# Attention in blocks of 64 tokens from the second batch on, another way out for the last outputs, and other priorities in the planner

## The chip, the cores and the metric

The kernel runs on one core of a Trainium2 chip. The core has a matrix engine (TensorE, PE in the rows; its weight loads are PEld), VectorE (DVE), ScalarE (ACT), GpSimd (POOL) and SyncE (SP), which issues transfers. Matrix products go to banks of PSUM, everything else is in SBUF. The metric is the device time of one launch in microseconds, on random inputs of the fixed shapes below. Lower is better.

## What is computed

Four batches of 768 tokens. A linear attention with decay over 8 heads of 48 gives x (384 columns), which goes through two small networks in a row. Cut to its core:

```python
# attention, per token t, state [B, H, 48, 48]
cur = einsum('bhd,bhe->bhde', u * k_t, v_t)
y_t = einsum('bhd,bhde->bhe', r_t, state + cur)
state = w[..., None] * state + einsum('bhd,bhe->bhde', k_t, v_t)
# first network
h = gelu(x @ w_in)                       # [B, 768, 1024]
u, v = h[..., :512], h[..., 512:]
v_n = layernorm(v) * g_ln
v_s = einsum('ts,bsd->btd', w_sg, v_n) + b_sg[None, :, None]
x2 = x + (u * v_s) @ w_out
# second network, conv over 5 tokens back
gate = sigmoid(sum(conv_w[k] * x2_padded[:, k:k+768] for k in range(5)))
out = (gate * (x2 @ w_val)) @ w_out2
```

## The kernel before

**Attention** goes through 24 chunks of 128 tokens (i = 0 to 23, six to a batch, NCH = 6). r is multiplied by the decay up to its token, k by its inverse, both are transposed (att_T, tiles rT and kT), then scores kT x rT are made and masked so that only earlier tokens count, and scores x v plus state x r give y. The term of the token itself, with u, is dv, a multiple of v. There are two forms of a chunk.

- *Plain* (i < QUAD = 12): scores for 128 tokens (L680) into two PSUM banks, masked by DVE (L690, two instructions) into two buffers "sc"; in att_Y the transpose of dv (L858), state x r (L864) and v x scores (L877) into one bank, copied out by ScalarE (L902); KV for the next state (L707), added by DVE (L716, L718).
- *In blocks of 64 tokens* (i >= QUAD): att_Yq makes state x r and v x scores (L842) for two half chunks in two banks, and at once the scores (S_blocks, L751) and KV (KV_blocks, L785) of the next chunk in two more. The diagonal with u is put into the score tile beforehand, and DVE copies the scores over it under a mask (L759, two instructions); y is copied out of two banks (L936) and two additions by DVE bring the parts together (L942). The states are then three tiles T2, which `states` lays into the two "sc" buffers once chunk QUAD - 1 is done, with memsets on GpSimd.

For chunks up to RAW - 1 = 12 r and k are transposed by TensorE (L654) into one bank each, and emptied by DVE (rT, L662) and ScalarE (kT, L660). From chunk 13 on DVE transposes them (L622).

**The networks** are lists of tasks per batch (V, U: the two halves of w_in with gelu; S: gate product with w_sg; O: w_out; A: w_val; P: w_out2). Every product is done three times with parts of high and low order (L1093, L1094, L1095). The weights come as double words and are made into such parts by `prepare`: a load by SP (L391), ScalarE (L379), three operations by DVE (L1419 on "words", L381, L382), a cast and a subtraction. For the first block of w_in these steps wait until the planner has placed a certain attention step: LATER holds a letter for each step, and `run_step` holds a step back until a step that has that letter in `opens` is placed.

**The order** of the instructions on each engine is written by a planner with a clock of its own. `go` takes TensorE's pieces of two streams (attention and network tasks), each with its price in ns, the results that it needs and the tokens it takes (TOKENS: four PSUM banks "pa" for attention, three "pm" for the networks, buffers for scores, weights, outputs). `choose` takes the attention as long as `done[0]`, the attention's price so far, is behind the networks' (times RATE); EXTRA is added to `done[0]` for a chunk in blocks. The work of the other engines is given as chains of steps with a priority (smaller goes first: pr(i) for attention, PR_V, PR_U and others for the networks), and `advance` places the step that can begin first. Where the planner sees TensorE idle before FILL_END, it puts in warm-up products (L222), FILL of the idle time. BODY0 and its like are the orders of the network tasks in a batch.

**The end.** An output is copied out of PSUM by ScalarE (L1270) and sent by SP (L1271). After the last, all engines load a count n_ok and branch on it (L1495, L1496) past a second program for unusual decays, which is not run here.

Of the kernel before, what the change touches and what calls it, by code (L numbers as in the profile page):

```python
# [17 lines left out]
P = 128  # L18
B, H, S, D = 4, 8, 768, 48
DM = H * D  # L20
FF = 512
NCH = S // P
# [10 lines left out]
class Kern:  # L33
# [498 lines left out]
    def att_new(self, i):  # L532
# [17 lines left out]
        free = [("KV", j) if j >= QUAD or j % NCH != NCH - 1 else ("T", j)] if j >= 0 else [("T", 0)] if i else []  # L550
        if i == 1:
            ks.opens = "b"
        self.chain(("kS", i), ("P", 956.0, ks), after=[("ld", i), "tabS"] + free, prio=pr(i))
# [88 lines left out]
    def att_T(self, i):  # L642

        nc = self.nc
        res = self.kr[i] = [None, None]
        for n, (src, tab, tag) in enumerate(((self.rp, self.tabR, "rT"), (self.ks, self.tabK, "kT"))):
# [17 lines left out]

            if i == 1 and not n:
                evac.opens = "a"
# [144 lines left out]
    def att_Yq(self, i):  # L811

        nc = self.nc
        c = i % NCH
        nxt = i + 1
        s = nxt < B * NCH
# [4 lines left out]
        )  # L821
        self.done[0] += EXTRA
        Z = [self.ps_a(), self.ps_a()]
# [26 lines left out]
    def att_Y(self, i):  # L850

        nc = self.nc
# [7 lines left out]
        if c:  # L860
# [5 lines left out]
        kv = i >= JOIN and c != NCH - 1  # L866
        s = i >= JOIN and i + 1 < B * NCH
        block = i + 1 >= QUAD
        yield (
            1000 + 390 * kv + (A_NS if block else 980) * s,  # L870
# [175 lines left out]
    def attention(self):  # L1046

        out = [self.att_T(0)]
        n = B * NCH
        for i in range(n):  # L1050
            step = {
                "S": ([self.att_S(i)] if i <= JOIN else []) + ([] if i else [self.tables_state()]),
                "K": [self.att_KV(i)] if i < JOIN and i % NCH != NCH - 1 else [],
                "T": [self.att_T(i + 1)] if i + 1 < min(n, RAW) else [],
                "Y": [self.att_Y(i) if i < QUAD else self.att_Yq(i)],
            }
            for k in ORDER:
                out += step[k]
        return out + [self.count()]
# [194 lines left out]
    def mlp_O2(self, b, half, q, dst=None):  # L1254
# [8 lines left out]
        if q == 2:  # L1263
            self.give("R", NC)
        t = self.Sx()
        r0 = half * TH + q * P
        out = self.out[b, r0:r0 + P, :] if dst is None else self.out[ds(dst, 1), r0:r0 + P, :].rearrange("o p n -> (o p) n")
        self.chain(
            ("o", b, half, q),
# [178 lines left out]
def pr(i):  # L1448

    return 0 if i < NCH else PR_A  # L1450


PR_A, PR_V, PR_V0, PR_U, PR_SG, PR_REST = 1, 0.05, -1, 0.2, 0.8, 2
PR_PS = 1
ORDER, JOIN = "SKTY", 6
A_NS, Y_NS, EXTRA = 1070, 530, 1000.0
RAW, PR_RAW = 13, 1
QUAD, PAST_NS = 12, 520
AFTER_SG, AFTER_SM, AFTER_CW = 6, 6, 9
# [7 lines left out]
TOKENS = {"R": NR, "W": NW, "S": NS, "A": NA, "xf": NX, "yT": NY, "sc": 2, "pw": 1, "pa": NPA, "pm": 7 - NPA}  # L1467
T_LD, T_R, T_K, T_S = 6000.0, 8300.0, 9000.0, 9000.0
V_FREE, A_FREE, P_FREE = 9000.0, 7700.0, 5000.0
# [3 lines left out]
HOLD = {"gelu": HOLD_G, "sigmoid": HOLD_S}  # L1473
FILL, FILL0 = 0.4, 0.8
FILL_END = 30000.0
FIRST = "V0 U00 V1 U01 V2 U02 V3 U03 V4 V5"
LAST = "U10 S00 U11 S01 U12 S02 U13 S03 O00 O01 O02 S10 S11 A00 A01 A02 S12 S13 P00 O10 P01 O11 P02 O12 A10 A11 A12 P10 P11 P12"
BODY0 = "U10 S00 U11 S01 U12 S02 U13 S03 O00 O01 O02 S10 S11 A00 A01 A02 S12 S13 P00 O10 P01 O11 P02 O12 v0 A10 u00 A11 v1 A12 u01 v2 u02 v3 u03 v4 P10 P11 P12 v5"
BODY = "U10 S00 U11 S01 U12 S02 U13 S03 O00 O01 O02 S10 S11 A00 A01 A02 S12 S13 P00 O10 P01 O11 P02 O12 v0 A10 u00 A11 v1 A12 u01 v2 u02 v3 u03 v4 P10 P11 P12 v5"
END = "U10 S00 U11 S01 U12 S02 U13 S03 O00 O01 O02 S10 S11 S12 S13 A00 A01 A02 O10 O11 O12 P00 P01 A10 A11 A12 P02 P10 P11 P12"  # L1480
LATER = ['a', 'a', 'a', 'a', 'b', 'b']
FILLS = {}
W_LEAST, W_MOST = 0.75, 1.0
N_OK = HR * NP
# [42 lines left out]
```

## Time and profile before

| | us |
|---|---|
| three runs | 438.59, 439.81, 439.81 (median 439.81) |
| the profiled execution | 439.16 |
| its span, first to last instruction | 437.5 |
| outside the span | 1.66 |

| engine | busy us | share of the span |
|---|---|---|
| TensorE | 417.7 | 95% |
| its weight loads | 353.9 | 81% |
| DVE | 349.5 | 80% |
| GpSimd | 207.7 | 47% |
| ScalarE | 205.9 | 47% |

The mean granted clock of TensorE is 0.992 of full speed. The shares are means over the whole span. The same busy times cut into stretches, and single instructions with their starts, are in the section of rows; times there are counted from the span's start.

### The profile page before, as it was taken

The numbers are of one execution on the slowest core, as the hardware profiler recorded it, in microseconds if no ns is written. First come the engines' busy times: TensorE is split into PE (matmuls) and PEld (weight loads), VectorE is DVE, ScalarE is ACT, GpSimd is POOL, SyncE is SP. The second block draws the span as 40 slices with busy tenths as digits, with TensorE's granted clock in tenths as the row PEclk, the third lists the DMA queues.
The fourth block names the chain that finished last, engine by engine and source line by source line (L and its number), as shares of the span: only waits on it lengthen the run. The fifth ranks groups of instructions, "written<-read, shape, count | busy, mean of one in ns | idle before, by whom it ended". The sixth has DMA issues, their size and how long they took to land.

```text
span 437.5 us, 10656 instructions
## 1 busy us (share of the span) xinstructions
PE 417.7 (95%) x4181; PEld 353.9 (81%) x4181; DVE 349.5 (80%) x722; ACT 205.9 (47%) x433; POOL 207.7 (47%) x246
## 2 busy tenths in 40 slices
PE   7887898999999999999999999899999999999993
PEld 7766796987887988977887998777879998685993
DVE  6689898999989679679899799975696684569890
ACT  2545778745554466642344398531232763013151
POOL 6767649442667347884687677520100353000000
PEclk9999999899999999999999999999999999999998
DMA  7999995998603446684567744521002001000012
GB/s 152 230 248 243 231 297 107 162 227 191 155 7 73 127 116 137 160 205 106 138 142 167 197 109 115 133 80 38 1 0 92 18 1 54 1 0 1 0 38 78
DMA packets 128952, 50.10 MB, mean 115 GB/s; under 512 B 90752, under 2 KB 126720, under 8 KB 128896
## 3 DMA queue, kind: packets, MB, share of 16 engines
q1 hardware_dynamic: 128896, 49.35, 46.6%
q8 instruction: 35, 0.57, 0.5%
q14 instruction: 21, 0.17, 0.1%
HBM read 37.54 MB, written 9.44 MB: 107 GB/s over the span
## 4 chain that ended last, share of the span: by engine, by line
PE 66%; DVE 18%; POOL 5%; issue 4%; ACT 3%; DMA 1%; SPq 1%; DVEq 0%; POOLq 0%; ACTq 0%
PE pm L1093 19%; PE pm L1095 19%; PE pm L1094 19%; PE pa L842 2%; DVE words L1214 2%; POOL dv L1419 2%; DVE sc L690 2%; DVE R L990 1%; DVE S L382 1%; DVE words L381 1%; DVE R L1419 1%; PE pa L751 1%; PE pa L680 1%; PE pa L864 1%; DVE words L1419 1%
## 5 line engine op out<-in xcount | busy, mean ns | idle before, releaser
L1093 PE MATMUL pm<-wsg,vh 128*128 128x384 f16 x192 | 62.9, 327 | 0.0
L1095 PE MATMUL pm<-wsg,vh 128*128 128x384 f16 x192 | 62.6, 326 | 0.0
L1094 PE MATMUL pm<-wsg,vh 128*128 128x384 f16 x192 | 62.6, 326 | 0.0
L1214 DVE SCALAR_TENSOR_TENSOR words<-xf,cw,words 128x384 f32<-128x384 f32 x72 | 44.4, 617 | 6.0 <-ACT words L1212 4.7
L1419 POOL TENSOR_TENSOR R<-S,R 128x384 fp32r<-128x384 f32 x20 | 20.2, 1014 | 57.6 <-DVE R L1419 34.3
L1419 POOL TENSOR_TENSOR ks<-kp,tabS 128x384 f32<-128x384 f32 x24 | 24.3, 1011 | 22.4 <-PE pa L785 10.7
L1093 PE MATMUL pm<-R,win 128*128 128x384 f32 x96 | 33.9, 353 | 0.0
L1093 PE MATMUL pm<-R,wout 128*128 128x384 f32 x96 | 33.2, 346 | 0.6 <-DVE S L1180 0.6
L1095 PE MATMUL pm<-R,win 128*128 128x384 f32 x96 | 32.3, 337 | 0.0
L1094 PE MATMUL pm<-R,wout 128*128 128x384 f32 x96 | 32.2, 336 | 0.0
L1094 PE MATMUL pm<-R,win 128*128 128x384 f32 x96 | 32.2, 335 | 0.0
L1095 PE MATMUL pm<-R,wout 128*128 128x384 f32 x96 | 32.1, 335 | 0.0
L1180 DVE SCALAR_TENSOR_TENSOR S<-pm,gs,b_bc 128x384 f32<-128x384 f32 x32 | 19.6, 612 | 15.4 <-PE pm L1095 15.4
L1150 ACT ACTIVATE S<-pm 128x384 f32<-128x384 f32 x32 | 15.6, 489 | 33.3 <-PE pm L1095 33.2
L1419 POOL TENSOR_TENSOR R<-xf,R 128x384 fp32r<-128x384 f32 x12 | 12.3, 1038 | 39.4 <-ACT R L1445 18.7
L1093 PEld LDWEIGHTS <-vh 128*128 128x128 f16 x192 | 18.8, 98 | 14.0 <-issue 2.5
L1093 PE MATMUL pm<-win,R 128*128 128x512 f32 x72 | 29.8, 414 | 0.0
L1095 PE MATMUL pm<-win,R 128*128 128x512 f32 x72 | 29.1, 404 | 0.1
L1094 PE MATMUL pm<-win,R 128*128 128x512 f32 x72 | 29.0, 403 | 0.0
L1095 PEld LDWEIGHTS <-vh 128*128 128x128 f16 x192 | 18.8, 98 | 12.6 <-DVE vh L1419 0.3
L1445 ACT CAST R<-S 128x384 fp32r<-128x384 f32 x32 | 16.1, 512 | 24.8 <-DVE S L1419 9.5
L1094 PEld LDWEIGHTS <-vh 128*128 128x128 f16 x192 | 18.9, 98 | 10.8
(192 smaller groups left out, 1234.0 us busy)
## 6 DMA issues: line engine op xcount, KB each, us to landing
rp<-in_r_dram SPq DMA_DIRECT2D x24, 192.0 KB, 3.3
kp<-in_k_dram SPq DMA_DIRECT2D x24, 192.0 KB, 3.6
v<-in_v_dram SPq DMA_DIRECT2D x24, 192.0 KB, 3.4
xd<-yT SPq DMA_DIRECT2D x48, 96.0 KB, 2.2
xf<-xd SPq DMA_DIRECT2D x24, 192.0 KB, 3.1
out_dram<-S SPq DMA_DIRECT2D x24, 192.0 KB, 2.1
raw<-in_r_dram SPq DMA_DIRECT2D x43, 96.0 KB, 3.2
raw<-in_k_dram SPq DMA_DIRECT2D x43, 96.0 KB, 2.4
```

The source lines that it names most:

```text
L381: lambda e: e.scalar_tensor_tensor(ci, h, -(2 ** 31), ci, ALU.bitwise_and, ALU.bitwise_or),
L382: lambda e: e.scalar_tensor_tensor(a, l, 29, ci, ALU.logical_shift_right, ALU.bitwise_or),
L690: e.tensor_mul(t, ps.rearrange("s (p t) -> s p t", t=P), mb)
L842: nc.tensor.matmul(Z[r][64 * a:64 * a + w, q * Q:(q + 1) * Q], lh, rh, start=banks[n] not in banks[:n], stop=banks[n] not in banks[n + 1:])
L1093: nc.tensor.matmul(ps, lh, rh, start=m == 0, stop=False)
L1094: nc.tensor.matmul(ps, lh, rl, start=False, stop=False)
L1095: nc.tensor.matmul(ps, ll, rh, start=False, stop=m == total - 1)
L1150: self.chain(("u", b, half, f), ("A", ("gelu", 371.0), lambda e: e.activation(t, pu[:, :TH], AF.Gelu_apprx_tanh), [], ["pm"]))
L1180: ("V", 529.0, lambda e: e.scalar_tensor_tensor(t, pg[:, :TH], self.gs[:, d:d + 1], self.b_bc[:, ts], ALU.mult, ALU.add), [], ["pm"]),
L1214: eng.scalar_tensor_tensor(t, row[:, j:j + TH], self.cw[:, e, j:j + 1], t, ALU.mult, ALU.add)
L1419: self.made.append(call(*a, **kw))
L1445: return "AV", {"A": 413.0, "V": 269.0}, lambda e: e.copy(dst, src()) if hasattr(e, "copy") else e.tensor_copy(dst, src()), [], list(give)
```

## The change

- QUAD goes from 12 to 6: the chunks 6 to 11 (the second batch) go in blocks too. Their r and k are still transposed by TensorE (RAW stays). `s` and att_S follow, so that chunk 5 makes the scores and KV of chunk 6.
- For chunks up to 11 that go in blocks, EXTRA1 = 1560 is added to `done[0]` in place of EXTRA.
- Other priorities: chunks 6 to 8 at 0.9 (before 1), chunks 9 to 11 at 2.5 (before 1), later ones at 0.9; PR_V, PR_V0, PR_U, PR_PS, PR_RAW, and T_K, the time at which the planner holds tabK for done.
- Start: LATER has the letter "a" throughout, and "a" is opened by the evacuation of chunk 0's kT in place of chunk 1's rT. FILL 0.6 in place of 0.4, up to 40 us in place of 30 us on the planner's clock.
- In BODY0 two tasks change places (O10 ahead of P00).
- End: the last three outputs are sent by ScalarE's own queue, behind its copy, and sixteen products of a constant go into a PSUM bank of the networks after the last real product.

```diff
-        if i == 1:
-            ks.opens = "b"
...
-            if i == 1 and not n:
+            if not i and n:
                 evac.opens = "a"
...
-        self.done[0] += EXTRA
+        self.done[0] += EXTRA if i >= RAW - 1 else EXTRA1
...
-        s = i >= JOIN and i + 1 < B * NCH
         block = i + 1 >= QUAD
+        s = (i >= JOIN or block) and i + 1 < B * NCH
...
-                "S": ([self.att_S(i)] if i <= JOIN else []) + ([] if i else [self.tables_state()]),
+                "S": ([self.att_S(i)] if i <= JOIN and i < QUAD else []) + ([] if i else [self.tables_state()]),
...
+        if b == B - 1 and half:
+            if q == 2:
+                pz = self.ps_m()
+                for _ in range(LAST_FILL):
+                    nc.tensor.matmul(pz[:, 0:P], self.onesb, self.onesb, start=True, stop=True)
+            self.chain(("o", b, half, q), ("A", 371.0, lambda e: e.copy(t, po[:, :DM]), [], ["pm"]), ("A", 340.0, lambda e: e.dma_start(out, t), [], ["S"]))
+            return
...
-    return 0 if i < NCH else PR_A
+    return 0 if i < NCH else PR_A if i >= 2 * NCH or i < FROM_B else PR_B
...
-PR_A, PR_V, PR_V0, PR_U, PR_SG, PR_REST = 1, 0.05, -1, 0.2, 0.8, 2
-PR_PS = 1
+PR_A, PR_V, PR_V0, PR_U, PR_SG, PR_REST = 0.9, -0.05, -0.5, 0.9, 0.8, 2
+PR_PS = 0.5
 ORDER, JOIN = "SKTY", 6
-A_NS, Y_NS, EXTRA = 1070, 530, 1000.0
-RAW, PR_RAW = 13, 1
-QUAD, PAST_NS = 12, 520
+A_NS, Y_NS, EXTRA, EXTRA1 = 1070, 530, 1000.0, 1560.0
+FROM_B, PR_B = 9, 2.5
+RAW, PR_RAW = 13, 1.5
+QUAD, PAST_NS = 6, 520
...
-FILL, FILL0 = 0.4, 0.8
-FILL_END = 30000.0
+FILL, FILL0 = 0.6, 0.8
+FILL_END = 40000.0
...
-LATER = ['a', 'a', 'a', 'a', 'b', 'b']
+LATER = ['a', 'a', 'a', 'a', 'a', 'a']
 FILLS = {}
+LAST_FILL = 16
```

Three places in the order of the instructions. First TensorE, one chunk of the second batch between products of the networks; ident is a unit matrix, so these are transposes, pa are banks of attention. Before:

```order
L654 MATMUL pa_1659<-ident,rp_124 112x128 x4
L654 MATMUL pa_1666<-ident,ks_129 112x128 x4
L858 MATMUL pa_1676<-ident,dv_137 112x128 x4
L864 MATMUL pa_1676<-rT_1451,T_141 112x128 x4
L877 MATMUL pa_1676<-sc_1501,v_1392 48x128
L877 MATMUL pa_1676<-sc_1513,v_1392 48x128
```

After (the code has moved by two lines, L840 is L842 of before; the rows go on in this manner to 32 products of this line, then 16 of scores and 16 of KV):

```order
L652 MATMUL pa_1399<-ident,rp_125 112x128 x4
L652 MATMUL pa_1406<-ident,ks_129 112x128 x4
L840 MATMUL pa_1420<-rT_1182,T_136_1024 64x64
L840 MATMUL pa_1421<-rT_1182,T_135_1023 64x64
L840 MATMUL pa_1420<-rT_1182,T_135_1023 64x64
L840 MATMUL pa_1421<-rT_1182,T_136_1024 64x64
L840 MATMUL pa_1420<-rT_1182,T_136_1024 48x64
L840 MATMUL pa_1421<-rT_1182,T_135_1023 48x64
```

The transpose of dv, the state's products and the scores' products of 128 columns in one bank have become products of 64 columns that take turns between two banks.

Second DVE at the start, behind the tables; rT and kT are chunk 0's transposes, dd and sc its diagonal and scores, "words", S and win the conversion of w_in, T a state. Before (in the changed code L1419 is L1424, L690 is L688 and L662 is L660):

```order
L662 TENSOR_TENSOR kT_294<-pa_271,tabK 112x512
L571 TENSOR_REDUCE dd_330<-dv_136 128x8
L690 TENSOR_TENSOR sc_344<-pa_306,mask 128x512
L690 TENSOR_TENSOR sc_353<-pa_307,mask 128x512
L662 TENSOR_TENSOR rT_361<-pa_346,tabR 112x512
L1419 TENSOR_SCALAR words<-words 128x384
L381 SCALAR_TENSOR_TENSOR words<-Rst_203,words 128x384
L382 SCALAR_TENSOR_TENSOR S_363<-Rst_203,words 128x384
L716 TENSOR_TENSOR T_140<-pa_412,T_141 48x4x48 x2
L662 TENSOR_TENSOR rT_443<-pa_426,tabR 112x512
L690 TENSOR_TENSOR sc_453<-pa_432,mask 128x512
```

After:

```order
L660 TENSOR_TENSOR kT_297<-pa_274,tabK 112x512
L1424 TENSOR_SCALAR words<-words 128x384
L381 SCALAR_TENSOR_TENSOR words<-Rst_203,words 128x384
L569 TENSOR_REDUCE dd_337<-dv_136 128x8
L382 SCALAR_TENSOR_TENSOR S_299<-Rst_203,words 128x384
L688 TENSOR_TENSOR sc_352<-pa_315,mask 128x512
L716 COPY T_141<-pa_343 48x4x48
L688 TENSOR_TENSOR sc_366<-pa_316,mask 128x512
L1424 TENSOR_SCALAR words<-words 128x384
L381 SCALAR_TENSOR_TENSOR words<-Rst_208,words 128x384
L382 SCALAR_TENSOR_TENSOR S_357<-Rst_208,words 128x384
L660 TENSOR_TENSOR rT_411<-pa_400,tabR 112x512
```

The conversion of the first block now begins behind kT of chunk 0 and lies between the diagonal and the scores; the second block's begins right behind these.

Third ScalarE at the end; S are output tiles. Before:

```order
L1270 COPY S_5785<-pm_5772 128x384
L1270 COPY S_5800<-pm_5787 128x384
L1270 COPY S_5813<-pm_5801 128x384
L1270 COPY S_5826<-pm_5814 128x384
L1495 TENSOR_LOAD n_ok
L1496 COMPARE_AND_BRANCH
```

After:

```order
L1275 COPY S_6007<-pm_5994 128x384
L1271 COPY S_6022<-pm_6009 128x384
L1271 DMA out_dram<-S_6022 128x384
L1271 COPY S_6035<-pm_6023 128x384
L1271 DMA out_dram<-S_6035 128x384
L1271 COPY S_6048<-pm_6036 128x384
L1271 DMA out_dram<-S_6048 128x384
L1502 TENSOR_LOAD n_ok
L1503 COMPARE_AND_BRANCH
```

The three transfers (DMA) were on SP's queue, and are now on ScalarE's, each behind its copy, ahead of the load of the count and the branch.

## Rows read from the trace of the kernel before

**Rows 1.** Busy time by stretch: start:end length, busy us by engine, clock, DMA share, GB/s

```profile
0.00:40.00 40.00, 33.83 (x440) 28.96 (x441) 30.55 (x70) 18.44 (x48) 28.55 (x47) 1.00 0.92 214
40.00:80.00 40.00, 34.87 (x266) 29.12 (x265) 36.91 (x84) 29.24 (x69) 25.83 (x31) 0.96 0.89 217
80.00:140.00 60.00, 59.88 (x512) 48.78 (x510) 54.39 (x103) 30.60 (x66) 32.06 (x35) 1.00 0.62 132
140.00:300.00 160.00, 158.39 (x2218) 136.19 (x2219) 133.60 (x281) 82.12 (x174) 100.39 (x109) 1.00 0.55 136
300.00:431.00 131.00, 130.78 (x750) 110.89 (x749) 94.08 (x188) 45.19 (x80) 20.86 (x26) 1.00 0.06 22
```

**Rows 2.** Instructions of line L858: duration ns, first and last start us, shape

```profile
L858 PE MATMUL pa<-ident,dv x48: 270/273/323, 13.0 to 150.3; 128*112 128x128 f32 x48
```

**Rows 3.** Timeline of PE, one plain chunk: start us, us, line, instruction

```profile
93.09 0.60 PE L858 MATMUL pa<-ident,dv 128*112 128x128 f32 x4
93.53 1.04 PE L864 MATMUL pa<-rT,T 112*112 112x128 f32 x8
94.50 1.08 PE L877 MATMUL pa<-sc,v 128*48 128x128 f32 x16
95.41 0.53 PE L707 MATMUL pa<-v,ks 128*48 128x48 f32 x16
95.87 1.16 PE L680 MATMUL pa<-rT,kT 48*128 48x128 f32 x16
96.96 0.34 PE L1093 MATMUL pm<-wsg,vh 128*128 128x384 f16 x1
```

**Rows 4.** Timeline of PE, one chunk in blocks

```profile
179.39 0.72 PE L842 MATMUL pa<-rT,T 48*64 48x64 f32 x32
179.91 0.66 PE L842 MATMUL pa<-dv,v 64*64 64x64 f32 x32
180.38 0.66 PE L751 MATMUL pa<-rT,kT 48*64 48x64 f32 x32
180.84 0.64 PE L785 MATMUL pa<-v,ks 64*64 64x48 f32 x32
181.41 0.50 PE L1093 MATMUL pm<-win,R 128*128 128x512 f32 x1
```

**Rows 5.** DVE by line and shape: xcount, busy us, mean ns, idle before

```profile
L690 DVE TENSOR_TENSOR sc<-pa,mask 128x512 f32<-128x512 f32 x24 | 16.1, 683 | 3.5 <-PE pa L680 3.3
...
L759 DVE COPY_PREDICATED dv<-mask,pa 128x256 f32<-128x256 int16 x24 | 10.3, 440 | 0.0
...
L942 DVE TENSOR_TENSOR yT<-pa,yT 112x128 f32<-112x128 f32 x22 | 5.9, 279 | 0.0
```

**Rows 6.** Transfers of 0 to 40 us: xcount, KB each, median us to landing

```profile
Rst<-in_moe_w_in_dram SPq DMA_DIRECT2D x8, 384.0 KB, 5.0
```

**Rows 7.** Instructions of line L222, the warm-up products

```profile
L222 PE MATMUL warm<-onesb x126: 217/219/314, 1.2 to 27.2; 128*128 128x128 bf16 x126
```

**Rows 8.** Timeline of PE at 74 us, with the idle time before and its releaser

```profile
74.34 0.65 PE L654 MATMUL pa<-ident,rp 128*112 128x128 f32 x4 [2.10 <-ACT yT L902]
```

**Rows 9.** Busy time of the stretch behind it, columns as in rows 1

```profile
75.70:79.20 3.50, 3.43 (x10) 2.25 (x9) 3.50 (x7) 3.50 (x9) 1.91 (x2) 0.51 0.95 209
```

**Rows 10.** Timeline of ACT, the last output's copy

```profile
430.81 0.48 ACT L1270 COPY S<-pm 128x384 f32<-128x384 f32 x1 [1.08 <-PE pm L1095]
```

**Rows 11.** Instructions of line L1271, the outputs' issues

```profile
L1271 SPq DMA_DIRECT2D out_dram<-S x24: 332/354/1839, 143.9 to 431.3; - x24
```

**Rows 12.** Transfers of 425 us to the end

```profile
out_dram<-S SPq DMA_DIRECT2D x4, 192.0 KB, 2.4
```

**Rows 13.** Waits of SP from 400 us: waited for, us, times, longest

```profile
SPq L1496 <- SPq L1496: 3.2, 1, 3.2
```

**Rows 14.** Instructions of line L1496, the last branch

```profile
L1496 SPq EVENT_SEMAPHORE  x8: 17/17/17, 435.5 to 436.1; - x8
...
L1496 PEldq COMPARE_BRANCH  x1: 3836/3836/3836, 428.1 to 428.1; - x1
```

More of the change, by code (lines that the diff above doesn't have):

```diff
@@ L1467 @@
 TOKENS = {"R": NR, "W": NW, "S": NS, "A": NA, "xf": NX, "yT": NY, "sc": 2, "pw": 1, "pa": NPA, "pm": 7 - NPA}
-T_LD, T_R, T_K, T_S = 6000.0, 8300.0, 9000.0, 9000.0
+T_LD, T_R, T_K, T_S = 6000.0, 8300.0, 9400.0, 9000.0
 V_FREE, A_FREE, P_FREE = 9000.0, 7700.0, 5000.0
@@ L1473 @@
 HOLD = {"gelu": HOLD_G, "sigmoid": HOLD_S}
-FILL, FILL0 = 0.4, 0.8
-FILL_END = 30000.0
+FILL, FILL0 = 0.6, 0.8
+FILL_END = 40000.0
 FIRST = "V0 U00 V1 U01 V2 U02 V3 U03 V4 V5"
 LAST = "U10 S00 U11 S01 U12 S02 U13 S03 O00 O01 O02 S10 S11 A00 A01 A02 S12 S13 P00 O10 P01 O11 P02 O12 A10 A11 A12 P10 P11 P12"
-BODY0 = "U10 S00 U11 S01 U12 S02 U13 S03 O00 O01 O02 S10 S11 A00 A01 A02 S12 S13 P00 O10 P01 O11 P02 O12 v0 A10 u00 A11 v1 A12 u01 v2 u02 v3 u03 v4 P10 P11 P12 v5"
+BODY0 = "U10 S00 U11 S01 U12 S02 U13 S03 O00 O01 O02 S10 S11 A00 A01 A02 S12 S13 O10 P00 P01 O11 P02 O12 v0 A10 u00 A11 v1 A12 u01 v2 u02 v3 u03 v4 P10 P11 P12 v5"
 BODY = "U10 S00 U11 S01 U12 S02 U13 S03 O00 O01 O02 S10 S11 A00 A01 A02 S12 S13 P00 O10 P01 O11 P02 O12 v0 A10 u00 A11 v1 A12 u01 v2 u02 v3 u03 v4 P10 P11 P12 v5"
 END = "U10 S00 U11 S01 U12 S02 U13 S03 O00 O01 O02 S10 S11 S12 S13 A00 A01 A02 O10 O11 O12 P00 P01 A10 A11 A12 P02 P10 P11 P12"
-LATER = ['a', 'a', 'a', 'a', 'b', 'b']
+LATER = ['a', 'a', 'a', 'a', 'a', 'a']
 FILLS = {}
+LAST_FILL = 16
 W_LEAST, W_MOST = 0.75, 1.0
```

## The prediction, made before the changed kernel was run

> **What bounds the kernel now.** I read the busy times by stretch first [rows 1], because the share over the whole span mixes stages with different limits. From 80 us on TensorE is busy for 59.88 of 60, 158.39 of 160 and 130.78 of 131 us: whatever shortens TensorE's own work there shortens the kernel, unless another engine then comes up behind it. From 0 to 80 us it has 33.83 and 34.87 of 40 us (the first with warm-up products in it), so there it waits for others. VectorE (DVE) is the one to look at: 36.91 of 40 us and 54.39 of 60 us between 40 and 140 us, 91.3 of 100 us in all. It drops to 133.60 of 160 and 94.08 of 131 behind that. So there are three regions: a start in which TensorE waits, 40 to 140 us in which both engines are nearly full, and the rest, which TensorE alone decides. The plain chunks that the change turns into blocks lie in the second region: the last plain chunk's transpose is at 150.3 us [rows 2].
>
> **TensorE's work in chunks 6 to 11.** The starts of the pieces of one plain chunk follow one another on TensorE [rows 3]: transpose of dv 0.44 (93.09 to 93.53), state 0.97, scores times v 0.91, KV 0.46, scores of the next chunk 1.09, together 3.87 us. A chunk in blocks [rows 4] has 0.52 for the past, 0.47 for its own products, 0.46 for scores, 0.57 for KV, together 2.02 us. An ordinary chunk saves 1.85 us. Chunks 7 to 10 are ordinary: 4 x 1.85 = 7.4. Chunk 6 is the first of its batch: before without the state (3.87 - 0.97 = 2.90), after with half of the past (2.02 - 0.26 = 1.76): 1.14. Chunk 11 is the last of its batch: before without KV (3.41), after with half of it (2.02 - 0.285 = 1.735): 1.67. The sum is 10.2 us, of which 8.5 lies in chunks 6 to 10 and 1.7 in chunk 11. The transposes of r and k stay as they are in both.
>
> **What of that gets through.** The 1.7 of chunk 11 comes at about 150 us, where DVE has room: counted whole. The 8.5 comes out of a stretch in which DVE's work hardly changes: per chunk two masked scores of 683 ns are replaced by two predicated copies of 440 and two additions of 279, 1.37 against 1.44 us [rows 5]; reductions and state additions stay. In 40 to 140 us DVE has 8.7 us without work. If all 8.5 were to come through, DVE would need 91.3 us of work in 91.5 us, without a gap. What gives room is that the planner can move DVE work behind 140 us, where DVE is busy for 84% of the time (133.60 of 160). Against this, the conversions, layernorm and gate of batches 0 and 1 that TensorE's products wait for are as many as they were. So the bounds are 0 (DVE decides) and 8.5 (TensorE decides), and no row lies nearer to one of them: DVE's idle time of 8.7 us would halve at the middle. I take 4.0 for everything up to 140 us.
>
> **The start.** The conversion of a first weight block now stands ahead of chunk 0's scores on DVE (the order above shows it), and two more weight loads stand ahead of chunk 1's. Two loads of 384 KB at the 214 GB/s of 0 to 40 us [rows 1, 6] are 3.7 us (786 KB by 214 GB/s) for which chunk 1's data comes later; the first MLP product's weights come earlier, and DVE has 40 - 30.55 = 9.45 us of idle time in that stretch. Later attention and earlier MLP work exchange places in a stretch where TensorE waits for either. Bounds: -3.7 (the MLP products fill idle TensorE time for as long as the loads took) to +3.7 (every later step waits for chunk 1). I take 0, since both come out of the same idle time; a gain at the start would be part of the 4.0. The order has 158 warm-up products where there were 126. The 32 new ones go into time that the planner holds to be idle; at 0.219 us each [rows 7] they cost 7.0 us at most, if TensorE had work in all of it, and nothing if it has none. DVE, DMA and TensorE's 33.83 of 40 us, of which the old ones are a part, speak for the lower end: I take nothing.
>
> **New waits.** An attention step in blocks takes all four PSUM banks of attention at once (two for the result, two for the next chunk), where a plain step gets by with one, then two or three. The rT and kT transposes of the same chunks want these banks too. So TensorE, which works in program order, can stop at such a step with the MLP products queued behind it. Nothing before shows this step together with such transposes. The nearest row is a wait of 2.10 us for ScalarE's copy out of PSUM at 74.34 us [rows 8], behind which the granted clock was 0.51 for 3.5 us [rows 9]; at the half level of 1.2 GHz that costs another 1.75 us. There is also the clearing of the states on GpSimd, which needs both score buffers once and now falls in the stretch that is full; its price is at most such a stall too. Bounds for both: -1.7 (the stall at 74 us itself goes, since its place is rearranged) to +3.85 a stall. I take +0.6, a third of one wait without the clock: the other four-bank steps, from chunk 12 on, ran with TensorE at 158.39 of 160 us.
>
> **The end.** The last copy starts at 430.81 us and takes 0.48 [rows 10]; SP issues the transfer at 431.3 [rows 11], and it lands 2.4 us after that, at 433.7 [rows 12]. But SP gets to its last branch only after this issue, and then stands 3.2 us [rows 13]; its semaphores come from 435.5 us on [rows 14], 1.8 us after the landing. With the last three issues on ScalarE's queue, SP gets to that branch three outputs earlier, 3 x (0.48 + 1.08) = 4.7 us [rows 10], and the 3.2 us lie beside the last products. ScalarE has 1.08 us idle ahead of such a copy [rows 10], and an issue takes about 0.35 [rows 11]: it fits. The sixteen dummies take 16 x 0.219 = 3.5 us [rows 7] of TensorE at most, less where they overlap, beside the last output's way out. TensorE's own branch, 3.84 us from 428.1 to 431.9 [rows 14], may slip by as much: up to a slip of 1.8 it is over when the data lands. ScalarE's branch comes after its last issue; whether it gets SP's stall no row tells. Bounds: 1.8 (all of it hidden) and 0 (ScalarE or TensorE stands as long as SP did). I take 1.3, since only one of these two would have to be hidden a little less than wholly for the half that I leave out.
> The Trainium skill, "Runtime: NRT & Kernel Launch", section "Instruction fetch mechanics", says that a taken branch to code outside the prefetched window waits for a fetch. SP's 3.2 us agree, but by this rule ScalarE's branch, once it is the last, would have the same wait, and the end would gain nothing.
>
> **Sum.** 4.0 + 1.7 + 1.3 - 0.6 = 6.4 us less than the profiled 439.16: **432.8 us**. The median of the runs is 0.65 above the profiled one. A change within 0.3% (1.3 us) can't be told from none here.
>
> **The rivals.**
> *TensorE decides everywhere.* All 10.2 come through, the end gives 1.3, and the stall at 74 us goes with its 1.7 of half clock: 439.2 - 13.2 = 426.0. For it: 99.8% from 80 us on, DVE's idle 8.7 us and its room after 140. Against it: it needs DVE without any gap.
> *DVE decides up to 140 us.* Nothing of the 8.5 comes through: 439.2 - 1.7 - 1.3 = 436.2. For it: 91.3 of 100 us, and a DVE price per chunk that is the same. Against it: 8.7 us of idle time and the work that moves back.
> The Trainium skill, "TensorEngine Tiling (Array Packing)", section "PSUM Bottleneck", has this mechanism: smaller tiles speed TensorE but not the evacuation of PSUM, which may become the bottleneck. The unchanged 1.4 us per chunk on DVE agrees with its first half; no run here shows the second yet.
> *The four-bank step stalls, slower.* Each of the six steps (chunks 6 to 11) can stop TensorE as at 74 us: 2.10 + 1.75 = 3.85 us. The whole gain is 10.2 + 1.3 = 11.5, so it decides from three stalls on (11.6); with four it is 15.4 - 11.5 = 3.9 slower: 443.1. For it: the transposes of these chunks use the same banks, and DVE, which empties them, is full. Against it: from 80 us on TensorE has found its plain steps' banks free nearly always (59.88 of 60).
> *The end does not do what it says.* The stall at the branch turns up on ScalarE or TensorE in SP's place, and the 1.3 are not gained: 439.2 - 5.1 = 434.1. For it: ScalarE's branch now comes last. Against it: SP's is the only long one of those that came late [rows 14].
>
> **How the numbers follow.** Forecast 0.42 (430 to 435), the end without its gain 0.08, TensorE everywhere 0.17, DVE decides 0.22 (435 to 438.2), stalls 0.11. The range leaves out the stalls above 438.2 (0.09) and the half of the TensorE case that would lie below its own time (0.08): 426.0 to 438.2. Faster by over 0.3% are the forecast, the case of the end, TensorE, and the DVE case but for a third, which with a first stall or two ends within 0.3%: 0.82; same 0.09; slower, three or more stalls, 0.09.
>
> **What would show it.** In the profile after: attention in 64-token products from chunk 6 on, and their pieces near 2.0 us; TensorE over 59 of 60 us still in 80 to 140 (TensorE case and forecast) or 55 or less beside a DVE of over 57 (DVE case); idle time of TensorE ahead of the step's first product, with a copy out of PSUM as the releaser and a granted clock near 0.5 behind it (stalls); the time from the start of the last output's copy to the end of the span, 437.5 - 430.8 = 6.7 us before, 5.4 after. It is wrong if DVE is not nearly full and TensorE waits all the same, or if the attention of batch 1 falls so late that batch 1's first MLP products wait for it.

## The result and the profile after

| | before | changed |
|---|---|---|
| first measurement, median (runs) | 439.65 us (4) | 435.32 us (4), 434.83 to 436.37 |
| ratio, 95% interval | | 0.9915, 0.9896 to 0.9934 |
| second measurement (e11), median (runs) | 439.92 us (17) | 438.33 us (12), 436.89 to 439.76 |
| ratio, 95% interval | | 0.9966, 0.9949 to 0.9983 |
| profiled execution, its span | 439.16, 437.5 us | 434.83, 433.0 us |

By the medians the kernel became faster by 4.3 us in the first measurement and by 1.6 in the second, by the ratios by 3.7 and 1.5. The two intervals do not meet. Neither of them holds "no change", so the sign is sure, and the size is not: somewhere from 0.7 to 4.6 us by the ends of the intervals, where 6.4 was forecast. Of all runs one, of e9 (453.62 us at a granted clock of 0.973), fell in a slower state of the chip and is left out of its time below. The traces that follow are those of the first measurement unless said otherwise.

The busy time of the changed kernel by stretch, in the columns of [rows 1]:

```profile
0.00:40.00 40.00, 34.95 (x448) 30.43 (x450) 29.46 (x68) 19.16 (x45) 27.20 (x44) 1.00 0.88 206
40.00:80.00 40.00, 36.28 (x413) 30.83 (x409) 36.59 (x93) 29.32 (x72) 28.98 (x37) 1.00 0.81 212
80.00:140.00 60.00, 55.37 (x846) 43.11 (x849) 53.16 (x109) 31.80 (x72) 34.72 (x37) 0.97 0.76 156
140.00:300.00 160.00, 158.04 (x2199) 134.48 (x2191) 130.97 (x284) 80.34 (x166) 98.85 (x105) 1.00 0.53 131
300.00:426.00 126.00, 126.00 (x723) 107.68 (x722) 92.97 (x185) 44.27 (x78) 20.85 (x26) 1.00 0.06 21
```

TensorE is busy for 55.37 of 60 us between 80 and 140 us, where it was 59.88: 4.5 us of new idle time. DVE is not busier there than before, 53.16 against 54.39. From 140 to 300 us both kernels are alike (158.04 and 158.39), and from 300 us on there is no gap.

The pieces of a chunk of the second batch (chunk 9), now in blocks, on TensorE, in the columns of [rows 3]:

```profile
119.47 0.72 PE L840 MATMUL pa<-rT,T 48*64 48x64 f32 x32
119.99 0.66 PE L840 MATMUL pa<-dv,v 64*64 64x64 f32 x32
120.45 0.66 PE L749 MATMUL pa<-rT,kT 48*64 48x64 f32 x32
120.92 0.64 PE L783 MATMUL pa<-v,ks 64*64 64x48 f32 x32
121.49 0.44 PE L1091 MATMUL pm<-R,w_val 128*128 128x384 f32 x1
```

From 119.47 to 121.49 it takes 2.02 us, to the hundredth as in [rows 4], against the 3.87 of [rows 3].

TensorE from 82 to 91 us, where most of the new idle time lies; in brackets the idle time before and its releaser:

```profile
82.08 0.34 PE L1093 MATMUL pm<-R,win 128*128 128x384 f32 x1
82.26 0.60 PE L652 MATMUL pa<-ident,rp 128*112 128x128 f32 x4
...
83.23 0.72 PE L840 MATMUL pa<-rT,T 48*64 48x64 f32 x32
83.74 0.66 PE L840 MATMUL pa<-dv,v 64*64 64x64 f32 x32
85.26 0.69 PE L749 MATMUL pa<-rT,kT 48*64 48x64 f32 x32 [0.86 <-DVE vh L1424]
85.77 0.63 PE L783 MATMUL pa<-v,ks 64*64 64x48 f32 x32
88.50 0.62 PE L652 MATMUL pa<-ident,rp 128*112 128x128 f32 x4 [2.09 <-issue]
...
89.39 0.33 PE L1091 MATMUL pm<-wsg,vh 128*128 128x384 f16 x1
90.01 0.48 PE L1092 MATMUL pm<-wsg,vh 128*128 128x384 f16 x1 [0.30 <-DMA wsg<-psg]
```

The last network product ahead of these steps is at 82.08. Then come, in program order, the transposes of chunk 8, the step of chunk 7 in blocks (results at 83.23, chunk 8's scores at 85.26, KV at 85.77), the transposes of chunk 9, and the first gate product. The next transposes wait 2.09 us for a bank, since the step has taken all four. The second gate product waits until 90.01 for the gate weights' last transfer. No network product lies between these steps.

The scores wait 0.86 us for kT. The row names a cast by DVE (vh) that ended at about the same time, but the product does not read it; kT's copy by ScalarE ends at 85.20. These are the steps that the copy stands behind:

```profile
82.97 0.55 POOL L1424 TENSOR_TENSOR rs<-rs,exps 128x1 f32<-128x1 f32 x1 [2.75 <-DVE psg L1424]
83.92 0.82 ACT L1122 ACTIVATE A<-A,nm,rs 128x512 f32<-128x512 f32 x1 [0.97 <-POOL nm L1424]
84.64 0.56 ACT L658 COPY kT<-pa 112x512 f32<-112x512 f32 x1
```

In ScalarE's row a layernorm step (L1122) is ahead of the copy and waits 0.97 us for GpSimd. GpSimd in turn began its part of that step only at 82.97, after 2.75 us of idle time that ended with DVE's conversion of the gate weights (psg, 79.26 to 82.89), a result which it does not read. DVE behind that:

```profile
86.28 0.57 DVE L1424 TENSOR_SCALAR words<-words 128x384 int32<-128x384 int32 x1 [0.59 <-ACT words L379]
...
87.23 0.56 DVE L381 SCALAR_TENSOR_TENSOR words<-Rst,words 128x384 int32<-128x384 int32 x1
87.69 0.35 DVE L793 TENSOR_TENSOR T<-pa,T 112x192 f32<-112x192 f32 x1
87.96 0.43 DVE L757 COPY_PREDICATED dv<-mask,pa 128x256 f32<-128x256 int16 x1
```

It works on conversions of weights ("words", wout) up to 87.69, then adds the state and copies the scores (L793 and L757, from bank to SBUF). The transposes begin at 88.50, just behind that copy, which ends at 88.39 (87.96 + 0.43). Behind the wait, the granted clock is 0.57 in 90 to 94 us, about 4 x 0.43 = 1.7 us of lost time, as after the wait at 74 us before ([rows 8, 9]), which is gone:

```profile
84.00:90.00 6.00, 2.77 (x103) 2.21 (x93) 5.41 (x15) 3.83 (x11) 3.72 (x4) 1.00 1.03 134
90.00:94.00 4.00, 3.99 (x15) 1.98 (x16) 3.68 (x4) 3.24 (x5) 1.40 (x2) 0.57 1.17 234
```

At the end, the last copy on ScalarE and the branch instructions (the columns of [rows 10] and [rows 14]):

```profile
427.29 0.48 ACT L1271 COPY S<-pm 128x384 f32<-128x384 f32 x1 [1.08 <-PE pm L1093]
427.79 0.34 ACTq L1271 DMA_DIRECT2D out_dram<-S  x1
```

```profile
L1503 SPq EVENT_SEMAPHORE  x8: 17/17/17, 426.9 to 431.6; - x8
...
L1503 SPq COMPARE_BRANCH  x1: 53/53/53, 424.1 to 424.1; - x1
L1503 PEldq COMPARE_BRANCH  x1: 3702/3702/3702, 427.6 to 427.6; - x1
L1503 ACTq COMPARE_BRANCH  x1: 54/54/54, 428.7 to 428.7; - x1
L1503 ACTq EVENT_SEMAPHORE  x1: 17/17/17, 429.2 to 429.2; - x1
```

The last output's transfer in the same trace (427.7 us to the end; the columns of [rows 12], the queue is ScalarE's now):

```profile
out_dram<-S ACTq DMA_DIRECT2D x1, 192.0 KB, 3.5
```

From the start of the last copy to the end of the span it is 433.0 - 427.29 = 5.7 us, where it was 6.7. SP reaches its branch at 424.1, beside the products, and its next instruction comes at 426.9: the stall is still there, 2.8 us, but lies beside other work. ScalarE's next instruction comes 0.5 us behind its branch (428.7 and 429.2), so it has no such stall. TensorE's branch takes 3.70 us, about as before (3.84), but starts at 427.6, behind the dummies, and ends at 431.3. The last output, issued at 427.79, takes 3.5 us to land, until 431.3 too, where it took 2.4 before. Branch and landing end together, so this trace does not tell which of them sets the end.

### The profile page after: what moved, and what is told of

Read it like the earlier page. It is cut to its first block, busy times and chain, and to the rows that moved or that the text cites. A ratio compares the mean times of both kernels' runs of the same rounds, so it can differ in the third digit from the quotient of the medians.

```text
span 433.0 us, 11603 instructions
## 1 busy us (share of the span) xinstructions
PE 412.8 (95%) x4629; PEld 348.3 (80%) x4629; DVE 343.2 (79%) x736; ACT 205.6 (47%) x432; POOL 210.6 (49%) x248
## 4 chain that ended last, share of the span: by engine, by line
PE 67%; DVE 12%; DMA 6%; POOL 6%; ACT 3%; issue 3%; SPq 3%; POOLq 0%; DVEq 0%; ACTq 0%
PE pm L1091 20%; PE pm L1092 20%; PE pm L1093 20%; PE pa L840 3%; DMA raw<-in_r_dram 2%; SPq L616 2%; POOL dv L1424 1%; PE pa L749 1%; DMA u_bc<-in_u_dram 1%; DVE R L988 1%; DMA wsg<-psg 1%; PE pa L783 1%; DVE words L1424 1%; POOL ks L1424 1%; DVE sc L688 1%
## 5 line engine op out<-in xcount | busy, mean ns | idle before, releaser
L1091 PE MATMUL pm<-wsg,vh 128*128 128x384 f16 x192 | 63.5, 331 | 0.9 <-DVE S L1242 0.9
L1092 PE MATMUL pm<-wsg,vh 128*128 128x384 f16 x192 | 63.4, 330 | 0.3 <-DMA wsg<-psg 0.3
L1093 PE MATMUL pm<-wsg,vh 128*128 128x384 f16 x192 | 63.4, 330 | 0.0
L1424 POOL TENSOR_TENSOR R<-S,R 128x384 fp32r<-128x384 f32 x19 | 19.1, 1009 | 60.8 <-DVE R L1424 37.6
L1424 POOL TENSOR_TENSOR ks<-kp,tabS 128x384 f32<-128x384 f32 x24 | 24.2, 1009 | 26.6 <-PE pa L783 13.4
L1424 POOL TENSOR_TENSOR R<-xf,R 128x384 fp32r<-128x384 f32 x14 | 14.5, 1036 | 41.5 <-ACT R L1450 20.9
L1093 PE MATMUL pm<-win,R 128*128 128x512 f32 x72 | 28.7, 399 | 1.7 <-DVE R L988 1.7
L1091 PE MATMUL pm<-win,R 128*128 128x512 f32 x72 | 28.8, 401 | 0.5 <-ACT R L984 0.5
L1092 PE MATMUL pm<-win,R 128*128 128x512 f32 x72 | 28.5, 396 | 0.0
```

Source lines behind the costliest of these rows:

```text
L1091: nc.tensor.matmul(ps, lh, rh, start=m == 0, stop=False)
L1092: nc.tensor.matmul(ps, lh, rl, start=False, stop=False)
L1093: nc.tensor.matmul(ps, ll, rh, start=False, stop=m == total - 1)
L1424: self.made.append(call(*a, **kw))
```

## Experiments

### e1 and e12: the end alone

The kernel before, with nothing but the change of the end; e12 leaves out the dummies.

```diff
+            self.chain(("o", b, half, q), ("A", 371.0, lambda e: e.copy(t, po[:, :DM]), [], ["pm"]), ("A", 340.0, lambda e: e.dma_start(out, t), [], ["S"]))
...
+LAST_FILL = 16   # e1; 0 in e12
```

> The kernel before with the change of the end alone: last three outputs by ScalarE's queue, sixteen dummy products. Theory (the end gives what the traces differ by there, 6.69 against 5.71 us from the last copy's start to the end of the span): 1.0 us faster than before, 438.6. Rival (nothing of it, the time is only moved between the queues): within 0.3 us of before.

Measured: 439.48 against 440.02 us, ratio 0.9982 (0.9962 to 1.0002), 0.8 us by the ratio. The interval, from a loss of 0.1 to a gain of 1.7 us, holds both the theory and the rival.

> The kernel before with the last three outputs by ScalarE's queue and no dummy products. Theory (the dummies push TensorE's last branch behind the last landing; without them the end, from the last copy's start, takes 4.1 us, as in the changed kernel without dummies, where it took 6.7 before and 5.6 with dummies): 2.6 us faster than before, 437.2 where before is 439.8, in an interval that leaves out no change. Rival (the end is worth as little as with dummies): 0.8 us faster or less.

Measured: 439.24 against 440.03 us, ratio 0.9992 (0.9970 to 1.0015): a loss of 0.7 to a gain of 1.3 us. The theory (2.6 us faster) was missed, and the rival came. The times from the last copy's start to the end of the span were 437.2 - 431.65 = 5.55 us in e1, and in e12 437.6 - 432.39 = 5.2, not the 4.1 of e2. The branches of e12:

```profile
L1504 SPq EVENT_SEMAPHORE  x8: 17/17/17, 431.9 to 435.1; - x8
...
L1504 PEldq COMPARE_BRANCH  x1: 3976/3976/3976, 429.7 to 429.7; - x1
...
L1504 ACTq COMPARE_BRANCH  x1: 54/54/54, 433.8 to 433.8; - x1
```

```profile
SPq L1531 <- PEq L1531: 1.6, 2, 1.4
```

Its last output's transfer:

```profile
out_dram<-S ACTq DMA_DIRECT2D x1, 192.0 KB, 1.9
```

TensorE's branch takes 3.98 us and ends at 433.7, ahead of the last landing. But at the closing semaphores (L1531) SP waits 1.6 us in all for TensorE's queue, where e1 has 0.6. The landing itself follows the dummies: in the five traces with them, in which TensorE's branch falls beside the last transfer, that takes 3.5, 3.4, 3.5, 3.7 and 3.8 us (the changed kernel, e1, e5, e7, e11), ending within 0.1 us of that branch, and 1.9 in the two without (e2 and e12). Why, no run shows. From the last copy's start to the end of the span it is 5.5 to 6.0 us in the five, and 4.1 and 5.2 in the two. So in the traces the dummies lengthen the end, while the measured times of e1 and e12 do not tell the two apart.

### e2: the changed kernel without dummies

```diff
-LAST_FILL = 16
+LAST_FILL = 0
```

> The changed kernel without the sixteen dummy products. Theory: in the changed kernel TensorE's last branch (3.70 us from 427.6) ends last, and it starts 0.3 us after the last real product where before it started 2.7 us ahead of it. Without the dummies it starts some 3 us earlier, and the last landing at about 430.1 decides: 1.1 to 1.3 us faster than the changed kernel, about 434.1. Rival (the dummies hold back a stall of the branch, or something else at the end follows them): within 0.3 us of the changed kernel, or slower.

Measured: 436.27 against 440.02 us (434.29 to 438.71), ratio 0.9909 (0.9873 to 0.9945). From the last copy to the end 432.5 - 428.41 = 4.1 us in its profile, 1.6 less than with dummies; the copy itself came 1.1 us later than in the first trace of the changed kernel, with the same order ahead of it. Its profile is of its fastest execution. Its ratio is that of the first measurement of the changed kernel (0.9915), which fits the rival, and its median is 2.1 us lower than that of e11 (the same chip, another series), which fits the theory. With e12 beside it I don't count a gain as shown.

### e3, e4 and e8: blocks and priorities, one without the other

e3 is the changed kernel with plain chunks up to 11; e4 is the kernel before with the blocks and EXTRA1 alone; e8 is the changed kernel with the old priorities.

```diff
 # e3, in the changed kernel
-QUAD, PAST_NS = 6, 520
+QUAD, PAST_NS = 12, 520
 # e4, in the kernel before
-QUAD, PAST_NS = 12, 520
+QUAD, PAST_NS = 6, 520
...
+        self.done[0] += EXTRA if i >= RAW - 1 else EXTRA1
 # e8, in the changed kernel
-PR_A, PR_V, PR_V0, PR_U, PR_SG, PR_REST = 0.9, -0.05, -0.5, 0.9, 0.8, 2
+PR_A, PR_V, PR_V0, PR_U, PR_SG, PR_REST = 1, 0.05, -1, 0.2, 0.8, 2
-FROM_B, PR_B = 9, 2.5
+FROM_B, PR_B = 9, 1
```

> The changed kernel with QUAD back at 12: chunks 6 to 11 plain, start, priorities and end as changed. Theory (the blocks carry the gain of 3.5 us ahead of the end, the start and the priorities next to nothing): slower than the changed kernel by 2.5 to 4.5 us, about 438.7. Rival 1 (start and priorities carry it, the blocks lose what they save): within 1.3 us of the changed kernel. Rival 2 (the new start and priorities cost, and the blocks gain more than is seen): over 440.

Measured: 447.68 against 440.02 us, ratio 1.016 (1.012 to 1.020).

> The kernel before with the blocks alone: QUAD 6, the code that goes with it and EXTRA1; start, priorities and end as before. Theory (the blocks carry the gain ahead of the end): 2.5 to 4.5 us faster than before, about 436.1. Rival 1 (without the new priorities DVE and the PSUM banks stall the blocks): within 1.3 us of before or slower. Rival 2 (the new priorities cost): 432 or less.

Measured: 458.0 against 440.02 us, ratio 1.040 (1.034 to 1.045).

> The changed kernel with all priorities as before (attention of the second batch at 1, and V, U, PS, RAW). Blocks, start, end and EXTRA1 as changed. Theory (the priorities are what keeps the four-bank steps from waiting for late rT, kT and v): 445 to 456, with waits of 2 to 4 us ahead of the scores in blocks. Rival (the start does that, or it takes both): below 440 or near the 458 of the blocks alone.

Measured: 456.2 against 439.16 us, ratio 1.039 (1.037 to 1.041).

Neither half of the change is worth anything alone. The priorities without the blocks (with the new start and end) cost 7.7 us, and the blocks without the priorities 17 to 18. In e3 the second rival held, in e4 the first. In e8 the time lies just above the theory's range and is as near to the rival's 458; that the old start takes no part is shown by e7 below, where the new priorities with the old start run at 438.4. The waits of TensorE in 80 to 160 us of e8 (waited for, us in total, times, longest) show what the blocks stall on:

```profile
PE pa L783 <- DMA v<-in_v_dram: 5.0, 3, 2.1
PE pa L749 <- POOL kT L1424: 3.7, 1, 3.7
PE pa L749 <- DVE rT L660: 1.8, 1, 1.8
PE pa L652 <- issue: 1.6, 1, 1.6
```

```profile
80.00:140.00 60.00, 48.79 (x885) 38.62 (x883) 51.13 (x108) 27.01 (x62) 33.61 (x34) 0.94 0.91 193
140.00:300.00 160.00, 151.48 (x1872) 128.05 (x1873) 125.34 (x273) 81.81 (x168) 103.11 (x109) 0.97 0.47 117
```

KV of the next chunk (L783) stands in the same step as this chunk's results, and its v has not landed (5.0 us in three waits); its scores (L749) stand there too, and kT is not yet weighed (3.7 us, at 142.36, in the step of chunk 12, which went in blocks before too). A step in blocks needs rT, kT, ks and v of the next chunk at once, and TensorE stops for the latest, with all products behind it. TensorE is busy for 48.79 of 60 us and 151.48 of 160, with half clock in places (0.94 and 0.97). The new priorities place the steps of chunks 9, 10 and 11 later: they begin at 119.47, 126.22 and 138.83 us in the changed kernel, and at 98.74, 109.54 and 118.45 in e8. These waits are gone then, and of the waits at steps in blocks in 80 to 140 us the two at 85 and 88 are left.

### e5 and e6: DVE relieved

Of the three DVE operations that convert a block of w_out, w_val or w_out2, two work on 16 of 384 columns; the other columns are left out, so these weights are wrong. On all five engines each instruction keeps its place.

```diff
-            lambda e: e.tensor_single_scalar(ci, ci, 3, op=ALU.logical_shift_left),
+            lambda e: e.tensor_single_scalar(ci[..., :n], ci[..., :n], 3, op=ALU.logical_shift_left),
```

> The changed kernel, every instruction in its place, but the first two of the three DVE operations that convert w_out, w_val and w_out2 work on 16 of 384 columns (these weights are wrong then; w_in's are not). Between 79 and 124 us DVE has eight such conversions: some 8 us of its work go there. Theory (DVE decides in that stretch and gives back what the blocks save): 2 to 5 us faster than the changed kernel. Rival 1 (the waits of TensorE are for something else, the gate weights' transposes by DMA or GpSimd): within 1.3 us of it. Rival 2 (the half clock behind the stall is all of the loss): 1.5 to 2 faster, with the stall gone.

Measured: 436.7 against 439.16 us (434.62 to 439.48), ratio 0.9951 (0.9925 to 0.9977), between the two measurements of the changed kernel itself.

> The kernel before with the same relief of DVE. Theory (TensorE decides there, and DVE has 5.6 us to spare in 80 to 140): within 1.3 us of before. Rival (DVE decided before too, the blocks only showed it): 2 to 5 us faster, as the changed kernel with the relief.

Measured: 438.68 against 439.16 us, ratio 0.9991 (0.9978 to 1.0004), as the theory had it: before, these conversions were not what held the kernel. TensorE and DVE in e5, then the waits of e5:

```profile
80.00:140.00 60.00, 55.82 (x897) 43.76 (x896) 47.08 (x110) 31.26 (x71) 35.57 (x37) 0.97 0.76 157
```

```profile
84.08 0.69 PE L749 MATMUL pa<-rT,kT 48*64 48x64 f32 x32 [0.84 <-ACT kT L658]
...
86.88 0.62 PE L652 MATMUL pa<-ident,rp 128*112 128x128 f32 x4 [1.65 <-issue]
...
88.67 0.48 PE L1092 MATMUL pm<-wsg,vh 128*128 128x384 f16 x1 [0.58 <-DMA wsg<-psg]
```

DVE has 6.1 us less to do than in the changed kernel between 80 and 140 us (47.08 against 53.16), and TensorE's busy time stays where it was, 55.82 of 60 (55.37, 55.60 and 54.47 in the three traces of the changed kernel's order, first, e2 and e11). The two waits are there again (0.84 and 1.65), the second one shorter; the whole stretch lies some 1.2 us earlier, and the gate weights come 1.3 earlier with it. The transposes at 86.88 again begin 0.1 us behind the end of DVE's first copy of the scores (86.34 to 86.78), and ahead of the end of GpSimd's ks (87.22), so the wait is for the bank. So the load of these conversions is not what TensorE waits for: each wait is a chain of single steps on several engines. DVE is not out of it, since e5 leaves the conversion of the gate weights as it was, and GpSimd's 2.75 us behind it are in this trace too; no run takes that away alone. My theory fell here, and with it the reason for the middle term of the sum.

### e9 and e10: the gate weights early

The scale of w_sg, which the sums over all of w_sg give, is put in as a constant, so that its conversion begins as soon as it is loaded. The planner then writes another order.

```diff
+        self.nc.gpsimd.memset(self.sc[:, 0:1], 65536.0)
...
-            prio=prio, after=["scale"] + ([("sg", 0, 0, 0)] if i >= 3 else []),
+            prio=prio, after=[("st", i)] + ([("sg", 0, 0, 0)] if i >= 3 else []),
```

> The changed kernel with the scale of the gate weights w_sg as a constant (65536, the value that it has for these inputs; the sums that give it are still made, but only the layernorm factor waits for them). The gate weights are converted and transposed as soon as they are loaded, and the planner puts gate products between the attention steps of chunks 8 and 9, where the changed kernel has none. Theory (from 81 to 90 us TensorE has only attention steps left, which wait for each other's PSUM banks, since the gate weights land at 89.9): the wait of 3.7 us in 80 to 90 and the half clock behind it go, 3 to 5 us faster than the changed kernel, 431 to 432. Rival 1 (another late input takes its place): within 1.3 us of it. Rival 2 (the four-bank steps stall wherever they stand): the same waits beside other products, no gain.

Measured: 446.79 against 439.92 us (three runs, 445.04 to 448.39), ratio 1.018 (1.013 to 1.022).

> The kernel before with the same constant scale. Theory (before, TensorE still had products when the gate weights came): within 1.5 us of before, or slower, as its priorities are not made for it. Rival (the gate weights held before up as well): 3 to 5 us faster.

Measured: 451.8 against 439.92 us, ratio 1.029 (1.025 to 1.032).

In e9 the theory's 3 to 5 us did not come; the second rival did, with a loss of some 7 us against before. In e10 the theory held (slower). The same kind of wait in e9 turned up ahead of the stretch, at 76.53, and new ones from 140 us on:

```profile
71.51 0.65 PE L784 MATMUL pa<-v,ks 64*64 64x48 f32 x32
76.53 1.07 PE L653 MATMUL pa<-ident,rp 128*112 128x128 f32 x4 [4.37 <-issue]
```

```profile
40.00:80.00 40.00, 32.41 (x388) 27.28 (x385) 33.04 (x72) 26.77 (x63) 28.01 (x35) 0.96 0.98 232
80.00:140.00 60.00, 56.86 (x906) 44.56 (x904) 57.24 (x134) 32.38 (x76) 37.15 (x39) 1.00 0.69 145
140.00:300.00 160.00, 151.41 (x2071) 129.15 (x2073) 132.23 (x277) 80.14 (x168) 93.04 (x101) 1.00 0.53 129
```

The transposes behind a step in blocks (KV at 71.51) wait 4.37 us for a bank, again until 0.1 us behind DVE's copy of the scores (75.99 to 76.42). TensorE is busy for 32.41 of 40 us in 40 to 80, where it was 36.28, and for 151.41 of 160 from 140 us on, where it was 158.04. In 80 to 140 us it is 56.86, 1.5 more than in the changed kernel. That the gate weights alone hold the stretch from 82 to 90 us is not borne out; since the whole order moved, it is not excluded either.

### e7: the old start

The changed kernel with LATER, its openers, FILL, FILL_END and T_K as before.

```diff
-LATER = ['a', 'a', 'a', 'a', 'a', 'a']
+LATER = ['a', 'a', 'a', 'a', 'b', 'b']
-FILL, FILL0 = 0.6, 0.8
-FILL_END = 40000.0
+FILL, FILL0 = 0.4, 0.8
+FILL_END = 30000.0
```

> The changed kernel with the start as before: the first weight conversions held back as before (LATER and what opens it), fewer warm-up products, the old time for tabK. Blocks, priorities and end as changed. Theory (the start is worth little, TensorE came to the same products 0.3 to 0.8 us earlier): within 1.5 us of the changed kernel. Rival (the new start is what keeps the blocks from stalling): over 440.

Measured: 438.4 against 439.16 us, ratio 0.9976 (0.9955 to 0.9997). The rival (over 440) fell: the new start is not what keeps the blocks from stalling: with the old one TensorE is busy for 55.65 of 60 us in 80 to 140, as in the changed kernel. By the ratios the start is worth 2.7 us beside the first measurement of the changed kernel and 0.4 beside the second; that it is worth something is not shown.

### e11: the changed kernel again

No edit.

> The changed kernel once more, unchanged, to have more runs of it beside before and beside the kernel without dummy products. Theory (the dummies cost 1.6 us at the end, and the scatter of the rest covers it): its median is 435 to 437.5, its spread as wide as that of the kernel without them (434.3 to 438.7). Rival (the dummies gain): its median is at or below 435.3 with a spread under 1.5 us.

Measured: 438.33 against 439.92 us, ratio 0.9966 (0.9949 to 0.9983). Theory and rival were missed: the median lies above 437.5, and the spread is 2.9 us. Its busy time of TensorE against the first trace of the same kernel:

```profile
80.00:140.00 60.00, 54.47 (x787) 42.70 (x789) 51.71 (x108) 31.12 (x70) 34.46 (x36) 0.97 0.72 149
140.00:300.00 160.00, 156.78 (x2243) 133.72 (x2232) 130.53 (x282) 80.78 (x167) 98.59 (x105) 1.00 0.54 131
```

It loses another 0.9 us in 80 to 140 and 1.3 in 140 to 300 us, and the last copy starts at 429.71 in place of 427.29. The waits at 85 and 88 us are the same in the first trace, e2 and e11 (0.85 to 0.87 and 2.08 to 2.10); others differ, as one of 1.7 us behind DVE's xf (L1198) that only e11 has in 80 to 140 us. The first trace is of the fastest of four executions (434.83 us), e2's of the fastest of six, e11's of a middling one (437.56). Three traces of the changed order up to the end (first, e2, e11) have the last copy at 427.3, 428.4 and 429.7; three of the order before (before, e1, e12) at 430.8, 431.7 and 432.4. Between the means lie 3.1 us: that is what blocks, priorities and start bring together, and the 3.5 of the first pair is one draw of it.

## Why the prediction was right in sign and range, and too large

- **The time**: the first measurement, 435.32, lies in the range of 426.0 to 438.2, the second, 438.33, 0.1 above it. Both lie where the rival "DVE decides" was put (435 to 438.2) or beyond, and not in the forecast's own 430 to 435; as e5 speaks against that rival's reason, that the time fell there is luck, and the range held by its width.
- **TensorE's work**: right. A chunk takes 2.02 in place of 3.87 us, so 10.2 us of work are gone.
- **What gets through**: the term that was mis-sized. For the part up to 140 us 4.0 less 0.6 for new waits were forecast, with 1.7 for chunk 11 behind it: 5.1 ahead of the end. The first pair of traces gives 430.81 - 427.29 = 3.5, the means of three 3.1. Of the 10.2 us, 4.5 are new idle time in 80 to 140 us, 0.35 in 140 to 300, and 1.7 the half clock in 90 to 94 us: 3.6 are left, which is the 3.5 measured. So ahead of 80 us about nothing is gained or lost on balance. TensorE is busy 2.5 us longer there, with 32 more warm-up products in it, and the wait and the half clock at 74 us are gone; no run tells the prices of these apart. I had priced the warm-up products at nothing.
- **The reason for that term**: wrong, and by the sign that the prediction had named for it: TensorE waits (55.37 of 60 us) while DVE is not nearly full (53.16). DVE's load was to decide in 40 to 140 us; e5 takes 6 us of it away with each instruction in its place and TensorE gets 0.45 us back there. A busy share of 91% of DVE was no bound; where DVE comes into the waits, it is by the place of single steps in its row. What held TensorE was named under the new waits and priced at 0.6: the step that takes all four banks. The wait of 2.09 us with 1.7 of half clock behind it and the 0.86 ahead of the scores make 4.7 us, but the wait of the same price at 74 us went, as the lower bound there allowed.
- **The rule on PSUM**: the second half of what the Trainium skill says in "TensorEngine Tiling (Array Packing)", section "PSUM Bottleneck", that the evacuation may become the bottleneck, agrees with the wait at 88.50, which ends with DVE's copy out of a bank; but the wait follows the place of that copy in DVE's row more than DVE's load, since 6 us less load shorten it only from 2.09 to 1.65 us (e5).
- **The four-bank rival**: its mechanism is what the blocks do with the old priorities (e4, e8: 17 to 18 us slower), though the longest waits are for v and kT and not for banks. The prediction gave the priorities no price of their own. They decide the sign.
- **The start**: taken as 0; e7 shows nothing that can be told from it.
- **The end**: 1.3 forecast, 1.0 in the first pair of traces, 0.7 in e11's, 0.8 in e1 with an interval from a loss of 0.1 to a gain of 1.7. That TensorE's branch may slip was given as a bound, free up to 1.8 us; behind the dummies it ends with the landing. That the landing itself takes 3.4 to 3.8 us beside that branch, where 2.4 was counted, the prediction did not have. ScalarE goes on 0.5 us behind its branch, where SP stands for 2.8. So the rule of the Trainium skill, "Runtime: NRT & Kernel Launch", section "Instruction fetch mechanics", under which the gain would have vanished there, does not show on ScalarE; whether ScalarE's branch leads outside its prefetched window no run tells. TensorE's 3.6 to 4.1 us in all kernels agree with it.

What stays open: what the stretch from 82 to 90 us would be worth without its waits. Had the bank been free at once, TensorE would have come to the gate products 2.1 us sooner, and these wait for their weights until 90.01 anyway; e9, which brought the weights early, moved the whole order. Open is also why the last landing is longer with the dummies, and what that costs in the measured time.

## What to carry to other kernels

A saving on the engine that is busy all the time comes through only as far as the order behind it has work ready: look at what is next in the row when the engine gets there earlier, not at the busy shares of the others. Joining steps saves work and gathers their inputs and banks in one place, so price the latest of these inputs for each joined step, and take the priorities that order the other engines' work, loads included, as part of the change: here they turned 17 us slower than before (e8) into 1.6 to 4.3 faster. A kernel of this kind needs several profiles and a second measurement before a difference of under 1% is given a size.

## What the runs showed that was not expected

With the old settings of the start e7 has 133 warm-up products (158 in the changed kernel, 126 before), and its granted clock in the first 40 us was 0.87, against 1.00 in both others. TensorE had been busy for 1.71 of 4 us from 16 to 20 us, and the clock was 0.56 and 0.50 in the next two stretches of 4 us, the lower of its two levels. The time hardly follows (438.4 against 438.33 in e11):

```profile
0.00:40.00 40.00, 34.80 (x388) 30.72 (x389) 28.50 (x65) 15.60 (x38) 24.78 (x42) 0.87 0.83 195
```

TensorE's last branch takes 3.84, 3.70, 3.58, 4.10 and 3.98 us (before, changed, e1, e2, e12), wherever it stands. SP's stall behind its own branch, 3.2 us before, is still there (2.8 us, from 424.1 to 426.9) when it is reached early, and costs nothing then.
